# Attention and two dense blocks in one kernel: sets of 384 tokens in place of 288 in the gated block

## The chip, the cores and the metric

The kernel runs on one core of one Trainium2 chip. The metric is the device time of one execution in microseconds; a kernel is timed in several runs, and one execution more is recorded by the hardware profiler, which gives the span from the first to the last instruction, the busy time of each engine and who waited for whom. PE is the matrix engine (PEld its weight loads), DVE, ACT and POOL are the vector, scalar and general engines, SP issues the transfers between the chip's memory and the on-chip buffers.

## What is computed

Attention over 4 batches of 576 tokens with 8 heads of 64, with a mask by blocks of 64 tokens, then two dense blocks on the 2304 x 512 result, all in float32:

```python
scores = scale * np.matmul(q, k.transpose(0, 1, 3, 2))
scores = np.where(mask, scores, -1000000000.0)
attn = softmax(scores)
x = (attn @ v).transpose(0, 2, 1, 3).reshape(B * S, H * D)
x = ((x @ w1) * (x @ w2)) @ w3 @ w_out                 # the gated block, 512 -> 1024 -> 1024 -> 512
h = x @ w_in                                           # the last block, 512 -> 2048 -> 512
out = np.where(h > 0, h, np.exp(np.minimum(h, 0)) - 1) @ w_out2
```

`mask[i, j]` is true where `i // 64 >= j // 64`.

## The kernel before, in words

Precision. A float32 operand is split in two parts for PE, a rounded one and the rest, and a product is made of three matmuls (`PASSES`: high with high, high with low, low with high). A split is a copy on ACT (or a cast on DVE) and a subtraction on POOL or DVE. Weights arrive as 64-bit words and are turned into float32 on ACT, DVE and POOL (`convert`).

Three stages, which overlap:

- *Attention* (`attention`): 16 pairs of heads, four for each batch. For a pair the scores of five groups of queries are made on PE, the maximum on DVE (L611), the exponential on ACT (L616), the transposition on PE (L626), the product with v on PE (L716). The sums' reciprocals go to the chip's memory and come back spread over the partitions as the tile `rr`, in three transfers (L758); POOL multiplies the pair's result, a part of `xy[b]`, by it (L770). `rr` has two buffers (`rr_r`).
- *The gated block* (`block2`). `w3 @ w_out` is multiplied once in advance (`w_product`, L786), so a set of tokens needs the two projections and one product. A set is `T2 = 288` tokens, half a batch; there are eight, and set t needs batch t // 2 alone. First the set's four slices of 128 features are cast and split into `xs` (DVE L827, POOL L832; one buffer, so the next set's `xs` waits for the last projection of this one). Then, for each of eight slices m of the 1024 features: 12 matmuls into `a`, copied by ACT (L899), 12 into `b`, multiplied by that copy on DVE (L904) and split into `g` (ACT L810, POOL L813). `g` has six buffers (`g2_r`). The output is summed in three parts over the slices, `PARTS = ((0,1,2),(3,4,5),(6,7))`: each part makes, for each of four slices n of the output, 3 matmuls for each of its m (L851). The first part is copied over the set's own place in `xy` (ACT L865), the others are added to it (DVE L871). Sets 0 to 2 have one PSUM bank for each of `a`, `b` and `y`, later ones two.
- *The last block* (`round_in`, `part_h`, `part_o`, `post`) works in three rounds of 768 tokens with Strassen's scheme: seven products of sums and differences of operand halves, in matmuls of `T3 = 384` columns (L1130 and L1208). `round_in(r)` makes the inputs `sy`; the result of `part_h` goes through the exponential unit into `ga` or `gb`; `part_o` builds sums of those (`sum_next`, three buffers), splits them (`split_next`, four places) and multiplies. There are six passes j; `part_o(j - 1)` is listed after `part_h(j)`, and the last `part_o` stands alone. Its weights were converted and stored to the chip's memory while the gated block ran.

Order. Nothing is issued directly. Each operation is added to a `Plan` with an engine (or several possible ones), an estimated duration, the buffers that it reads and writes and a priority. `Plan.run` is a list scheduler: it takes for each engine the operation that is ready and has the lowest priority, and issues in that order; the engines run their queues in order and wait for each other by semaphores. Attention's priorities lie below those of the gated block (base `1e4 + 1000 t`), and those below the last block's (`1e5`). The table `TURNS` replaces the priority of some operations, by their number, with values set by hand. Estimated durations, among them the cost of a matmul after one of another kind, the rate of the transfers and whether DVE and POOL hold each other up (`port`), decide the order alone, not what is computed.

Memory that is shared: `gate1` opens the buffers of the last block when attention and the conversions of the gated block's weights are done, `gate2` when the gated block is.

Of the kernel before, what the change touches and what calls it, by code (L numbers as in the profile page):

```python
# [29 lines left out]
T2 = 288  # L30
T3 = 384
BIG = 2.0**100
PARTS = ((0, 1, 2), (3, 4, 5), (6, 7))
# [106 lines left out]
class Op:  # L140
    __slots__ = ("eng", "ways", "us", "fn", "prio", "deps", "n", "ready", "end", "users", "left", "lag", "nbytes", "big")


class Plan:
    LANES = 8
    OVER = {"GATE": 0.0, "PE": 0.0, "DVE": 0.085, "ACT": 0.1, "POOL": 0.04}
    SEEN = {"GATE": 0.0, "PE": 0.055, "DVE": 0.035, "ACT": 0.035, "POOL": 0.08, "SP": 0.03}
# [4 lines left out]
    def add(self, eng, us, fn, r=(), w=(), prio=0.0, port=False, after=(), lag=0.0, nbytes=0, ways=(), big=False):  # L152

        o = Op()
        o.eng, o.us, o.fn, o.prio, o.lag, o.nbytes, o.big = eng, us, fn, prio, lag, nbytes, big
# [33 lines left out]
    def run(self):  # L189
# [11 lines left out]
        was_big = False  # L201
        pipe, port, done, lanes = 0.0, {"DVE": 0.0, "POOL": 0.0}, 0, [0.0] * self.LANES
        while done < len(self.ops):
# [15 lines left out]
            if e == "PE":  # L219
                o.us += 0.09 if o.big and not was_big else 0.0  # L220
                was_big = o.big
# [29 lines left out]
def attention_moe_moe2(  # L251
# [23 lines left out]
    N2, N3 = B * S // T2, B * S // (2 * T3)  # L275
    plan = Plan()
# [186 lines left out]
    rr_r = Ring(pool1, "rr", 2, [P, S], F32)  # L463
# [21 lines left out]
    def attention(n, first_op):  # L485
# [62 lines left out]
        def q_last():  # L548
# [8 lines left out]
            "POOL", 0.6, q_last, r=[(qs, 0)] if whole else [(qs, 0), (qs, 1)], w=[("qb", n % 2)], prio=pr + 1  # L557
# [14 lines left out]
        def group(g, seq):  # L572
# [7 lines left out]
            def scores():  # L580
# [20 lines left out]
                "PE", (4 * w / 2390 if whole else 3 * w * COL) + (0.28 if added else 0.17), scores,  # L601
                r=[*q_keys, *k_keys, "mask"], w=[*sb], prio=pg,
            )
            for h in range(2):
# [23 lines left out]
                add("PE", 0.11 * (g + 1) + 0.09, transposes, r=[p, "ident"], w=[t], prio=pg)  # L628
# [8 lines left out]
        def last_block(seq):  # L637
# [4 lines left out]
            for g in range(2):  # L642

                def scores(g=g):
# [13 lines left out]
                    "PE", (4 * kw / 2390 if whole else 3 * kw * COL) + 0.1, scores,  # L658
                    r=[("qb", n % 2), *k_keys], w=[sb[g]], prio=pg,
# [7 lines left out]
                )  # L667
            add(
                "DVE", 0.16, lambda: nc.vector.tensor_tensor(out=nm(10), in0=nm(8), in1=nm(9), op=ALU.min),
                r=[(st, "nm", 8), (st, "nm", 9)], w=[(st, "nm", 10)], prio=pg,  # L670
            )
            for g in range(2):
                add(
# [290 lines left out]
    def sum_next():  # L964
        b = sums[count("sum", 3)]
        return (lambda: b()[:, :]), (b, 0)
# [514 lines left out]
```

## Time and profile before

| | |
|---|---|
| median of 3 runs | 932.31 us (928.55, 932.61, 932.31) |
| the profiled execution | 929.41 us |
| its span | 927.6 us, 16695 instructions |
| PE, PEld | 901.3 us (97%), 799.0 us (86%) |
| DVE, ACT, POOL | 739.8, 513.2, 533.1 us |
| granted TensorE clock, mean | 0.996 of full speed |

The profile's page gives the busy time of each engine and the costliest groups of instructions: line, engine, operation, what it writes and reads, shape, count, then busy time, mean duration of one, and the idle time before them with what ended it. Matmuls are pipelined, so the records of neighbours overlap. The windows give the same busy times for a stretch of the span. The waits list who waited for whom. The chain follows the work that ended last back from the end, piece by piece.

### The profile page before, as it was taken

To read this page: it belongs to the slowest core of one execution; us is meant where nothing else is said; L and a number is where in the kernel's file an instruction comes from. 1 tells how busy PE (TensorE), PEld (TensorE's weight loads), DVE (VectorE), ACT (ScalarE), POOL (GpSimd) and SP (SyncE) were. 2 spreads that over 40 slices of the span, in tenths; PEclk is the share of its full clock that TensorE was granted. 3 is DMA by queue.
4 is the path that set the end of the run, shared out by engine and by line. 5 is a ranking of instruction groups with operands and counts; after the bars stand their busy time and mean duration, and the time that the engine had idled before them with its cause. 6 is when DMAs were issued, how large, how long until landed. Compare 5 with 4: busy or idle time off the path is not lost.

```text
span 927.6 us, 16695 instructions
## 1 busy us (share of the span) xinstructions
PE 901.3 (97%) x5838; PEld 799.0 (86%) x5838; DVE 739.8 (80%) x1450; ACT 513.2 (55%) x1190; POOL 533.1 (57%) x527
## 2 busy tenths in 40 slices
PE   7998899999999999999999999999999999999997
PEld 3454477888787778999999999999999999999996
DVE  7999889778676675777877768878998789986887
ACT  5857668666565654436354443455644547444552
POOL 6556667554242313578887985336995238961245
PEclk9999999999999999999999999999999999999999
DMA  8765553545222212777666595776789766887665
GB/s 267 242 203 172 171 159 97 180 148 167 79 73 67 69 39 88 249 253 251 219 220 215 170 308 193 232 262 234 247 287 304 264 223 216 308 285 269 213 199 188
DMA packets 100756, 186.24 MB, mean 201 GB/s; under 512 B 8512, under 2 KB 50496, under 8 KB 100672
## 3 DMA queue, kind: packets, MB, share of 16 engines
q1 hardware_dynamic: 100672, 185.18, 61.2%
q8 instruction: 46, 0.75, 0.3%
q14 instruction: 38, 0.31, 0.1%
HBM read 147.85 MB, written 37.30 MB: 200 GB/s over the span
## 4 chain that ended last, share of the span: by engine, by line
PE 71%; DMA 10%; DVE 8%; POOL 4%; issue 3%; ACT 3%; SPq 0%; POOLq 0%; DVEq 0%; ACTq 0%
PE y L851 9%; PE a L887 9%; PE b L887 8%; PE hx L1130 7%; PE ox L1208 7%; PE hz L1130 5%; PE hy L1130 5%; PE oy L1208 5%; PE oz L1208 5%; PE o L716 3%; PE s L590 3%; PE t L626 3%; DMA cr<-w 2%; DMA cr<-w3T 2%; DMA rr<-scr 2%
## 5 line engine op out<-in xcount | busy, mean ns | idle before, releaser
L851 PE MATMUL y<-g,slab_lo 128*128 128x288 f32 x768 | 120.2, 299 | 2.0 <-POOL g L813 2.0
L887 PE MATMUL a<-xs,slab_lo 128*128 128x288 f32 x768 | 117.6, 298 | 0.4 <-ACT af L899 0.3
L887 PE MATMUL b<-xs,slab_lo 128*128 128x288 f32 x768 | 116.7, 297 | 0.4 <-DVE af L904 0.4
L851 PEld LDWEIGHTS y<-g,slab_lo 128*128 128x128 f32 x768 | 107.4, 188 | 3.9 <-POOL g L813 2.2
L887 PEld LDWEIGHTS a<-xs,slab_lo 128*128 128x128 f32 x768 | 106.5, 188 | 2.0 <-ACT af L899 1.0
L887 PEld LDWEIGHTS b<-xs,slab_lo 128*128 128x128 f32 x768 | 106.5, 188 | 1.3 <-DVE af L904 0.6
L1208 PE MATMUL ox<-sp,wout 128*128 128x384 f32 x432 | 86.1, 335 | 0.9 <-DVE sum L1013 0.5
L616 ACT ACTIVATE p<-s,st 128x128 f32<-128x128 f32 (+3 forms) x128 | 67.4, 528 | 35.2 <-DVE st L611 26.7
L1130 PE MATMUL hx<-sy,win 128*128 128x384 f32 x432 | 86.5, 335 | 0.3 <-DVE ga L1013 0.3
L813 POOL TENSOR_TENSOR g<-af,g 128x288 fp32r<-128x288 f32 x64 | 57.6, 902 | 42.4 <-ACT g L810 40.4
L1208 PEld LDWEIGHTS ox<-sp,wout 128*128 128x128 f32 x432 | 75.7, 188 | 1.7 <-ACT sp L1003 0.8
L1130 PEld LDWEIGHTS hx<-sy,win 128*128 128x128 f32 x432 | 75.6, 188 | 1.0 <-DVE ga L1013 0.9
L1003 ACT CAST sp<-sum 128x384 fp32r<-128x384 f32 x72 | 36.7, 513 | 62.6 <-PE ox L1208 24.3
L786 PE MATMUL wps<-full,full 128*128 128x512 f32 x128 | 61.3, 613 | 4.5 <-DVE slab_lo L800 2.6
L611 DVE TENSOR_REDUCE st<-s 128x1 f32<-128x128 f32 (+3 forms) x128 | 61.9, 488 | 4.0 <-PE s L596 0.7
L384 ACT ACTIVATE cr<-cr 128x512 int32<-128x512 uint32 x72 | 49.0, 682 | 28.4 <-DMA cr<-w 19.8
L626 PE MATMUL t<-ident,p 128*128 128x128 f32 x320 | 56.3, 285 | 7.3 <-ACT p L616 4.9
L1208 PE MATMUL oy<-sp,wout 128*128 128x384 f32 x288 | 59.1, 336 | 1.5 <-DVE sp L1004 1.5
L626 PEld LDWEIGHTS t<-ident,p 128*128 128x128 f32 x320 | 37.3, 141 | 26.5 <-ACT p L616 13.5
L1130 PE MATMUL hz<-sy,win 128*128 128x384 f32 x288 | 57.6, 335 | 0.3 <-DMA win<-wsi 0.3
L1208 PE MATMUL oz<-sp,wout 128*128 128x384 f32 x288 | 57.1, 335 | 0.8 <-POOL sp L1004 0.8
L1130 PE MATMUL hy<-sy,win 128*128 128x384 f32 x288 | 57.6, 334 | 0.0
(154 smaller groups left out, 2093.7 us busy)
## 6 DMA issues: line engine op xcount, KB each, us to landing
wout<-wso SPq DMA_DIRECT2D x84, 512.0 KB
cr<-w SPq DMA_DIRECT2D x48, 512.0 KB
win<-wsi SPq DMA_DIRECT2D x24, 1024.0 KB
win<-wsi SPq DMA_DIRECT2D x24, 768.0 KB
cr<-w3T SPq DMA_DIRECT2D x16, 512.0 KB
wsi<-wh SPq DMA_DIRECT2D x8, 896.0 KB
wsi<-wt SPq DMA_DIRECT2D x8, 896.0 KB
wso<-wh SPq DMA_DIRECT2D x8, 896.0 KB
```

What stands on the lines that cost most here:

```text
L384: nc.scalar.activation(out=low, in_=low.bitcast(U32), func=AF.Copy, scale=2.0**-29)
L590: nc.tensor.matmul(sb[h]()[:, 0:w], lhsT=qs()[r, a, g * P:(g + 1) * P], rhs=ks()[r, c, 0:w], start=(x == 0), stop=(x == 2 and not added),)
L611: nc.vector.tensor_reduce(out=nm(c), in_=s()[:, 0:nk], axis=AX.X, op=ALU.max, negate=True)
L616: lambda s=s, c=c, p=p: nc.scalar.activation(out=p()[:, 0:nk], in_=s()[:, 0:nk], func=AF.Exp, bias=nm(c), scale=1.0, accum_out=sm(c)),
L626: nc.tensor.transpose(d[:, j, :], p()[:, j * P:(j + 1) * P], ident)
L786: nc.tensor.matmul(ps(), lhsT=a[:, j, :], rhs=bb, start=(j == 0), stop=(j == KF - 1))
L813: lambda: nc.gpsimd.tensor_tensor(out=g()[:, 1, :], in0=src(), in1=g()[:, 0, :].bitcast(F32), op=ALU.subtract),
L851: nc.tensor.matmul(ps()[:, 0:T2], lhsT=w[:, a, n * P:(n + 1) * P], rhs=gs[m]()[:, c, :], start=(m == ms[0] and q == 0), stop=(m == ms[-1] ...
L887: nc.tensor.matmul(ps()[:, 0:T2], lhsT=w[:, a, u, k, :], rhs=xs()[:, k, c, :], start=(k == 0 and q == 0), stop=(k == KD - 1 and q == 2),)
L1003: add("ACT", act_us(n, True), lambda: nc.scalar.copy(dst(0), src()), r=keys, w=[dkeys[0]], prio=prio)
L1130: nc.tensor.matmul(bk()[:, 0:T3], lhsT=w[:, a, k, :], rhs=s_(c), start=(first and k == 0 and i == 0), stop=(k == 1 and i == 2), skip_group ...
L1208: nc.tensor.matmul(to[n]()[:, 0:T3], lhsT=w[:, a, n * P:(n + 1) * P], rhs=sp(c), start=(first and q == 0 and i == 0), stop=(q == KP - 1 an ...
```

## The change

Sets of 384 tokens: `T2` is 384, there are six sets, and a set that spans two batches (the second and the fifth) is handled in two pieces for its inputs and for its outputs' copies and additions. `PARTS` becomes `((0,1,2),(3,4),(5,6,7))`, the ring of `g` has four buffers, `rr` one, `sums` two; sets 0 and 1 are now those with single banks. Before the last `part_o`, `widen` hands it ten more places for splits, in the slabs of `sy`, and eight more for sums. The planner knows six kinds of matmul and a cost for each change of kind, a lower transfer rate, and three more operations that hold the port; `TURNS` is replaced by a new table.

```diff
-T2 = 288
+T2 = 384
 T3 = 384
-PARTS = ((0, 1, 2), (3, 4, 5), (6, 7))
+PARTS = ((0, 1, 2), (3, 4), (5, 6, 7))
...
 TURNS = {
-    5: -2500.01, 24: -2400.0, 26: -10019.0, 31: -2542.64, 32: -9968.45, 51: -2496.99, 56: -871.07, 57: -10149.67,
...
+    4: -2505.56, 9: -100000.02, 22: -9857.07, 23: -997.98, 36: -3035.53, 41: -2498.87, 65: -2417.38, 69: -2499.99,
...
+    KINDS = {"": 0, "big": 1, "w": 2, "t": 3, "s": 4, "pv": 5, "qb": 6}
+    TURN = (
+        (0, 0, 0, 0, 0, 0, 0),
+        (0, 0, 0, 0.03, 0.085, 0.085, 0.03),
+        (0, 0, 0, 0, 0.094, 0.094, 0.03),
+        (0, -0.08, 0.04, 0.02, 0.14, 0.14, -0.08),
+        (0, 0, 0, 0, 0, 0, 0),
+        (0, 0, 0, 0, 0, 0, 0),
+        (0, 0.01, 0.01, 0, 0.09, 0.09, 0.05),
+    )
...
             if e == "PE":
-                o.us += 0.09 if o.big and not was_big else 0.0
-                was_big = o.big
+                o.us += 0.09 if o.kind in (1, 2) and last not in (1, 2) else 0.0
+                t = max(free[e] + self.TURN[last][o.kind], o.ready)
+                last = o.kind
...
-                pipe = max(pipe, t + 1.8) + o.nbytes / 325e3
+                pipe = max(pipe, t + 1.8) + o.nbytes / 300e3 + 0.05
...
-    rr_r = Ring(pool1, "rr", 2, [P, S], F32)
+    rr_r = Ring(pool1, "rr", 1, [P, S], F32)
...
-    g2_r = Ring(pool2, "g", 6, [P, 2, T2], F32R)
+    g2_r = Ring(pool2, "g", 4, [P, 2, T2], F32R)
...
     def block2(t):
-        b, h2 = divmod(t, 2)
-        c0 = T2 * h2
+        parts = pieces(t)
         xs = xs2_r.next()
-        base = 1e4 + 1000.0 * t
+        base = 1e4 + 1350.0 * t
         fast = -1e4 + t
-        x = xy[b]
         for k in range(KD):
-            src = lambda k=k: x()[:, k, c0:c0 + T2]
...
+            for b, o, n, d0 in parts:
+                x = xy[b]
+                src = lambda k=k, x=x, o=o, n=n: x()[:, k, o:o + n]
+                dst = lambda c, k=k, n=n, d0=d0: xs()[:, k, c, d0:d0 + n]
...
         gs = []
-        few = t < 3
+        few = t < 2
...
-                d = lambda n=n: x()[:, n, c0:c0 + T2]
-                dk = (x, n, "y", h2)
...
+                for b, o, cn, d0 in parts:
+                    x = xy[b]
+                    d = lambda n=n, x=x, o=o, cn=cn: x()[:, n, o:o + cn]
+                    acc = lambda ps=ps, d0=d0, cn=cn: ps()[:, d0:d0 + cn]
+                    dk = (x, n, "y", t)
...
-    sums = [Ring(late1, f"sum{u}", 1, [P, T3], F32, "gate1").next() for u in range(3)]
+    sums = [Ring(late1, f"sum{u}", 1, [P, T3], F32, "gate1").next() for u in range(2)]
...
+    def widen():
+        sx = [
+            chain([f"slab{s}"], "sx", [P, 2, 2, T3], F32R, [b]).next() for s, b in zip((11, 6, 7, 4, 5), sy_s)
+        ]
+        late["sx"] = [(b, u) for b in (*late["sp"], *sx) for u in range(2)]
+        su = [chain(b_tags, "sx", [P, 2, T3], F32, [b], late1, "gate1").next() for b_tags, b in zip(SY_TAGS, sy_l)]
+        late["su"] = [(b, u) for b in su for u in range(2)]
+
     def split_next():
+        if "sx" in late:
+            b, u = late["sx"][count("sx", len(late["sx"]))]
+            return (lambda c: b()[:, u, c, :]), [(b, u, c) for c in range(2)]
...
     def sum_next():
-        b = sums[count("sum", 3)]
+        k = count("su", len(late["su"]) + 2) if "su" in late else 0
+        if k >= 2:
+            b, u = late["su"][k - 2]
+            return (lambda: b()[:, u, :]), (b, u)
+        b = sums[count("sum", 2)]
...
         if j:
             part_o(j - 1)
+    widen()
     part_o(NP * N3 - 1)
```

`pieces(t)`, which the last block had already, cuts the 384 tokens of a set at the border between batches:

```python
def pieces(t):
    a0, found = t * T3, []
    while a0 < (t + 1) * T3:
        b, o = divmod(a0, S)
        n = min(S - o, (t + 1) * T3 - a0)
        found.append((b, o, n, a0 - t * T3))
        a0 += n
    return found
```

## Rows read from the trace of the kernel before

**Rows 1.** The page: each engine's busy time, share of the span, instructions.

```profile
PE 901.3 (97%) x5838; PEld 799.0 (86%) x5838; DVE 739.8 (80%) x1450; ACT 513.2 (55%) x1190; POOL 533.1 (57%) x527
```

**Rows 2.** Windows: stretch, length, busy time of each engine, clock, transfers.

```profile
core 0: us, PE busy (x) PEld busy (x) DVE busy (x) ACT busy (x) POOL busy (x), PEclk, DMA share, GB/s
0.00:125.60 125.60, 113.31 (x531) 57.85 (x531) 108.96 (x215) 85.83 (x200) 77.02 (x85) 0.97 0.67 207
125.60:243.00 117.40, 113.83 (x865) 97.14 (x863) 97.46 (x228) 78.39 (x208) 64.36 (x64) 1.00 0.44 140
243.00:365.00 122.00, 121.30 (x941) 95.92 (x940) 82.80 (x248) 72.20 (x217) 33.98 (x45) 1.00 0.21 63
365.00:893.00 528.00, 524.24 (x3358) 521.88 (x3355) 424.98 (x725) 264.15 (x541) 339.65 (x320) 1.00 0.74 244
403.40:559.00 155.60, 153.25 (x1142) 152.31 (x1141) 116.52 (x181) 74.54 (x144) 132.60 (x126) 1.00 0.72 232
750.00:800.00 50.00, 48.59 (x277) 47.58 (x276) 46.67 (x81) 28.67 (x66) 35.70 (x38) 1.00 0.75 258
893.00:927.60 34.60, 28.58 (x155) 26.21 (x153) 25.61 (x36) 12.64 (x26) 18.07 (x16) 0.99 0.63 203
```

**Rows 3.** The page's groups: the gated block's matmuls, count, busy, mean, idle before.

```profile
L851 PE MATMUL y<-g,slab_lo 128*128 128x288 f32 x768 | 120.2, 299 | 2.0 <-POOL g L813 2.0
L887 PE MATMUL a<-xs,slab_lo 128*128 128x288 f32 x768 | 117.6, 298 | 0.4 <-ACT af L899 0.3
L887 PE MATMUL b<-xs,slab_lo 128*128 128x288 f32 x768 | 116.7, 297 | 0.4 <-DVE af L904 0.4
```

**Rows 4.** The chain in order of time: start, length, what, matmuls in it.

```profile
379.74 3.20 PE b L887 x24
...
588.67 2.08 PE hx L1130 x12
```

**Rows 5.** Groups by shape, DVE, ACT and POOL: the gated block's own.

```profile
L904 DVE TENSOR_TENSOR af<-b,af 128x288 f32<-128x288 f32 x64 | 28.8, 452 | 20.9 <-PE b L887 16.0 <-ACT af L899 4.4
...
L810 ACT CAST g<-af 128x288 fp32r<-128x288 f32 x64 | 27.5, 432 | 34.5 <-DVE af L904 32.5 <-PE y L851 1.6
...
L813 POOL TENSOR_TENSOR g<-af,g 128x288 fp32r<-128x288 f32 x64 | 57.6, 902 | 42.4 <-ACT g L810 40.4 <-DVE sy L1004 1.8
L832 POOL TENSOR_TENSOR xs<-xy,xs 128x288 fp32r<-128x288 f32 x32 | 27.1, 865 | 8.7 <-DVE xs L827 8.6
```

**Rows 6.** Timeline of PE, 402 to 412 us: start, length, what.

```profile
403.19 6.59 PE L851 MATMUL y<-g,slab_lo 128*128 128x288 f32 x48
409.62 0.96 PE L887 MATMUL a<-xs,slab_lo 128*128 128x288 f32 x6
```

**Rows 7.** Timeline of POOL, 402 to 412 us.

```profile
405.23 2.11 POOL L1375 TENSOR_TENSOR wt<-wt,wh 128x256 fp32r<-128x256 f32 x2
407.30 1.56 POOL L832 TENSOR_TENSOR xs<-xy,xs 128x288 fp32r<-128x288 f32 x2
```

**Rows 8.** The normalizations (L770): duration least, median, most; first and last start.

```profile
L770 POOL TENSOR_TENSOR xy<-xy,rr x16: 1409/1422/1737, 47.5 to 365.9; 128x576 f32<-128x576 f32 x16
```

**Rows 9.** Waits of PE, 893 to 927.6 us: total, times, longest.

```profile
PE oy L1208 <- DVE sp L1004: 1.5, 3, 1.0
PE ox L1208 <- DVE sum L1013: 0.5, 1, 0.5
PE ox L1208 <- DVE sp L1004: 0.4, 1, 0.4
```

**Rows 10.** Timeline of PE, 122 to 128 us: the gated block's first matmuls.

```profile
125.59 1.84 PE L887 MATMUL a<-xs,slab_lo 128*128 128x288 f32 x12
```

**Rows 11.** Timeline of POOL, 234 to 244 us: the normalization of pair 7.

```profile
237.11 1.42 POOL L770 TENSOR_TENSOR xy<-xy,rr 128x576 f32<-128x576 f32 x1 [6.49 <-DVE st L611]
```

**Rows 12.** Groups of PE between 125.6 and 243 us: the gated block's matmuls.

```profile
L887 PE MATMUL a<-xs,slab_lo 128*128 128x288 f32 x174 | 27.2, 299 | 0.4 <-ACT af L899 0.3
L887 PE MATMUL b<-xs,slab_lo 128*128 128x288 f32 x174 | 26.5, 299 | 0.0
L851 PE MATMUL y<-g,slab_lo 128*128 128x288 f32 x132 | 22.7, 303 | 0.0
```

More of the change, by code (lines that the diff above doesn't have):

```diff
@@ L140 @@
 class Op:
-    __slots__ = ("eng", "ways", "us", "fn", "prio", "deps", "n", "ready", "end", "users", "left", "lag", "nbytes", "big")
+    __slots__ = ("eng", "ways", "us", "fn", "prio", "deps", "n", "ready", "end", "users", "left", "lag", "nbytes", "kind")
 class Plan:
@@ L150, in __init__, with add @@
         self.ops, self.writer, self.readers, self.filler = [], {}, {}, None
-    def add(self, eng, us, fn, r=(), w=(), prio=0.0, port=False, after=(), lag=0.0, nbytes=0, ways=(), big=False):
+    def add(self, eng, us, fn, r=(), w=(), prio=0.0, port=False, after=(), lag=0.0, nbytes=0, ways=(), kind=""):
         o = Op()
-        o.eng, o.us, o.fn, o.prio, o.lag, o.nbytes, o.big = eng, us, fn, prio, lag, nbytes, big
+        o.eng, o.us, o.fn, o.prio, o.lag, o.nbytes, o.kind = eng, us, fn, prio, lag, nbytes, self.KINDS[kind]
         o.ways = {e: x for e, *x in ((eng, us, fn, port), *ways)}
@@ L200, in run @@
                     ready[e].append(o)
-        was_big = False
+        last = 0
         pipe, port, done, lanes = 0.0, {"DVE": 0.0, "POOL": 0.0}, 0, [0.0] * self.LANES
@@ L275, in attention_moe_moe2 @@
     N2, N3 = B * S // T2, B * S // (2 * T3)
+    assert T2 == T3
     plan = Plan()
@@ L556, in attention @@
         add(
-            "POOL", 0.6, q_last, r=[(qs, 0)] if whole else [(qs, 0), (qs, 1)], w=[("qb", n % 2)], prio=pr + 1
+            "POOL", 0.6, q_last, r=[(qs, 0)] if whole else [(qs, 0), (qs, 1)], w=[("qb", n % 2)], prio=pr + 1, port=True
         )
@@ L600, in group @@
             add(
-                "PE", (4 * w / 2390 if whole else 3 * w * COL) + (0.28 if added else 0.17), scores,
-                r=[*q_keys, *k_keys, "mask"], w=[*sb], prio=pg,
+                "PE", (4 * w / 2390 if whole else 3 * w * COL) + (0.28 if added else 0.21), scores,
+                r=[*q_keys, *k_keys, "mask"], w=[*sb], prio=pg, kind="s",
             )
@@ L626, in transposes @@
                         nc.tensor.transpose(d[:, j, :], p()[:, j * P:(j + 1) * P], ident)
-                add("PE", 0.11 * (g + 1) + 0.09, transposes, r=[p, "ident"], w=[t], prio=pg)
+                add("PE", 0.109 * (g + 1), transposes, r=[p, "ident"], w=[t], prio=pg, kind="t")
                 pt = pts[g // 2]
@@ L657, in last_block @@
                 add(
-                    "PE", (4 * kw / 2390 if whole else 3 * kw * COL) + 0.1, scores,
-                    r=[("qb", n % 2), *k_keys], w=[sb[g]], prio=pg,
+                    "PE", (4 * kw / 2390 if whole else 3 * kw * COL) + 0.09, scores,
+                    r=[("qb", n % 2), *k_keys], w=[sb[g]], prio=pg, kind="qb",
                 )
@@ L669, in last_block @@
                 "DVE", 0.16, lambda: nc.vector.tensor_tensor(out=nm(10), in0=nm(8), in1=nm(9), op=ALU.min),
-                r=[(st, "nm", 8), (st, "nm", 9)], w=[(st, "nm", 10)], prio=pg,
+                r=[(st, "nm", 8), (st, "nm", 9)], w=[(st, "nm", 10)], prio=pg, port=True,
             )
@@ L686, in tr4 @@
                     nc.tensor.transpose(d[:, j, :], p()[:, j * P:(j + 1) * P], ident)
-            add("PE", 0.48, tr4, r=[(p, 0), (p, 1), "ident"], w=[t], prio=pg)
+            add("PE", 0.436, tr4, r=[(p, 0), (p, 1), "ident"], w=[t], prio=pg, kind="t")
             evac(
@@ L694, in last_block @@
             add(
-                "PE", 0.16, lambda: nc.tensor.transpose(t1()[0:D, 0:P], p()[:, 512:576], ident),
-                r=[(p, 1), "ident"], w=[t1], prio=pg,
+                "PE", 0.109, lambda: nc.tensor.transpose(t1()[0:D, 0:P], p()[:, 512:576], ident),
+                r=[(p, 1), "ident"], w=[t1], prio=pg, kind="t",
             )
@@ L723, in pv @@
                 r += [(pt, "q"), pts[2], (vt, 1)]
-            add("PE", (0.8, 2.3)[c], product, r=r, w=[o], prio=pg)
+            add("PE", (0.8, 2.353)[c], product, r=r, w=[o], prio=pg, kind="pv")
             x = xy[b]
@@ L745, in attention @@
         add("POOL", 0.15, lambda: nc.gpsimd.memset(st()[:, 41:64], 0.0), w=[(st, "rest")], prio=pr)
-        add("DVE", 0.85, recip, r=[(st, "rest"), *((st, "sm", c) for c in range(10))], w=[(st, "rs"), rs], prio=pr + 6)
+        add("DVE", 0.85, recip, r=[(st, "rest"), *((st, "sm", c) for c in range(10))], w=[(st, "rs"), rs], prio=pr + 6, port=True)
         def keep_sums(b):
@@ L789, in w_product @@
                 "PE", 0.86, mm,
-                r=[full_keys(W3_S, i % RW)[j // 4], full_keys(WO_S, j // 2)[j % 2]], w=[ps], prio=prio, big=True,
+                r=[full_keys(W3_S, i % RW)[j // 4], full_keys(WO_S, j // 2)[j % 2]], w=[ps], prio=prio, kind="w",
             )
@@ L805, in attention_moe_moe2, with pieces @@
     xs2_r = Ring(pool2, "xs", 1, [P, KD, 2, T2], F32R)
-    g2_r = Ring(pool2, "g", 6, [P, 2, T2], F32R)
+    g2_r = Ring(pool2, "g", 4, [P, 2, T2], F32R)
     a2_r = Ring(pool2, "af", 2, [P, T2], F32)
+    def pieces(t):
+        a0, found = t * T3, []
+        while a0 < (t + 1) * T3:
+            b, o = divmod(a0, S)
+            n = min(S - o, (t + 1) * T3 - a0)
+            found.append((b, o, n, a0 - t * T3))
+            a0 += n
+        return found
     def split_g(g, src, key, n, prio):
@@ L817, in block2 @@
     def block2(t):
-        b, h2 = divmod(t, 2)
-        c0 = T2 * h2
+        parts = pieces(t)
         xs = xs2_r.next()
-        base = 1e4 + 1000.0 * t
+        base = 1e4 + 1350.0 * t
         fast = -1e4 + t
-        x = xy[b]
         for k in range(KD):
-            src = lambda k=k: x()[:, k, c0:c0 + T2]
-            add(
-                "DVE", 0.32, lambda k=k, src=src: nc.vector.tensor_copy(xs()[:, k, 0, :], src()),
-                r=[(x, k, "n")], w=[(xs, k, 0)], prio=fast, port=True,
-            )
-            add(
-                "POOL", 0.79,
-                lambda k=k, src=src: nc.gpsimd.tensor_tensor(
-                    out=xs()[:, k, 1, :], in0=src(), in1=xs()[:, k, 0, :].bitcast(F32), op=ALU.subtract
-                ),
-                r=[(x, k, "n"), (xs, k, 0)], w=[(xs, k, 1), (x, k, "s", h2)], prio=fast, port=True,
-            )
+            for b, o, n, d0 in parts:
+                x = xy[b]
+                src = lambda k=k, x=x, o=o, n=n: x()[:, k, o:o + n]
+                dst = lambda c, k=k, n=n, d0=d0: xs()[:, k, c, d0:d0 + n]
+                add(
+                    "DVE", 0.15 + n * 0.00052, lambda src=src, dst=dst: nc.vector.tensor_copy(dst(0), src()),
+                    r=[(x, k, "n")], w=[(xs, k, 0, d0)], prio=fast, port=True,
+                )
+                add(
+                    "POOL", 0.17 + n * 0.00215,
+                    lambda src=src, dst=dst: nc.gpsimd.tensor_tensor(
+                        out=dst(1), in0=src(), in1=dst(0).bitcast(F32), op=ALU.subtract
+                    ),
+                    r=[(x, k, "n"), (xs, k, 0, d0)], w=[(xs, k, 1, d0), (x, k, "s", t)], prio=fast, port=True,
+                )
         gs = []
-        few = t < 3
+        few = t < 2
         abanks, bbanks, ybanks = ((5,), (6,), (7,)) if few else ((5, 0), (6, 1), (7, 3))
@@ L858, in y_part @@
                         r=[(gs[m], 0), (gs[m], 1), *((slab_buf[W_S + m // 2], y, m % 2) for y in range(2))],
-                        w=[ps], prio=base + (46, 90, 95)[part] + n, lag=LAG, big=True,
+                        w=[ps], prio=base + (46, 90, 95)[part] + n, lag=LAG, kind="big",
                     )
-                d = lambda n=n: x()[:, n, c0:c0 + T2]
-                dk = (x, n, "y", h2)
-                if part == 0:
-                    add(
-                        "ACT", act_us(T2), lambda d=d, ps=ps: nc.scalar.copy(d(), ps()[:, 0:T2]),
-                        r=[ps], w=[dk, (x, n, "s", h2)], prio=fast,
-                    )
-                else:
-                    add(
-                        "DVE", dve_us(T2),
-                        lambda d=d, ps=ps: nc.vector.tensor_tensor(out=d(), in0=ps()[:, 0:T2], in1=d(), op=ALU.add),
-                        r=[ps], w=[dk], prio=fast,
-                    )
+                for b, o, cn, d0 in parts:
[3 more added lines that the diff above has]
+                    dk = (x, n, "y", t)
+                    if part == 0:
+                        add(
+                            "ACT", act_us(cn), lambda d=d, acc=acc: nc.scalar.copy(d(), acc()),
+                            r=[ps], w=[dk, (x, n, "s", t)], prio=fast,
+                        )
+                    else:
+                        add(
+                            "DVE", dve_us(cn),
+                            lambda d=d, acc=acc: nc.vector.tensor_tensor(out=d(), in0=acc(), in1=d(), op=ALU.add),
+                            r=[ps], w=[dk], prio=fast,
+                        )
         for m in range(KF):
@@ L892, in proj @@
                     add(
-                        "PE", 6 * T2 * COL + 0.025, mm, r=[*wk, *((xs, k, c) for k in (k0, k0 + 1) for c in range(2))],
-                        w=[ps], prio=pr, lag=LAG, big=True,
+                        "PE", 6 * T2 * COL + 0.01, mm, r=[*wk, *((xs, k, c, p_[3]) for k in (k0, k0 + 1) for c in range(2) for p_ in parts)],
+                        w=[ps], prio=pr, lag=LAG, kind="big",
                     )
@@ L925, in attention_moe_moe2 @@
     win_r = slabs((8, 9, 10), "win", [P, 4, 2, NH], F32R)
+    SY_TAGS = [[f"sy{u}_0"] for u in range(4)]
     sy_l = [Ring(late1, f"sy{u}", 1, [P, 2, T3], F32R, "gate1").next() for u in range(4)]
     sy_s = [slabs((s,), "sy", [P, 2, 2, T3], F32R).next() for s in (11, 6, 7, 4, 5)]
-    sums = [Ring(late1, f"sum{u}", 1, [P, T3], F32, "gate1").next() for u in range(3)]
+    sums = [Ring(late1, f"sum{u}", 1, [P, T3], F32, "gate1").next() for u in range(2)]
     wout_r = Ring(late1, "wout", 4, [P, 2, 2, NH], F32R, "gate1")
@@ L943, in stage3 @@
         late["cp"] = xy_buf(0, "cp", (P, 6, T3))
-        late["n"] = dict.fromkeys(("sp", "sum", "ht"), 0)
+        late["n"] = dict.fromkeys(("sp", "sum", "ht", "sx", "su"), 0)
     def count(name, n):
-        late.setdefault("n", dict.fromkeys(("sp", "sum", "ht"), 0))
+        late.setdefault("n", dict.fromkeys(("sp", "sum", "ht", "sx", "su"), 0))
         late["n"][name] += 1
         return (late["n"][name] - 1) % n
+    def widen():
[5 more added lines that the diff above has]
+        late["su"] = [(b, u) for b in su for u in range(2)]
     def split_next():
+        if "sx" in late:
+            b, u = late["sx"][count("sx", len(late["sx"]))]
+            return (lambda c: b()[:, u, c, :]), [(b, u, c) for c in range(2)]
         k = count("sp", 4)
@@ L990, in sy @@
         return (lambda c: b()[:, kt, c, :]), [(b, kt, c) for c in range(2)]
-    def pieces(t):
-        a0, found = t * T3, []
-        while a0 < (t + 1) * T3:
-            b, o = divmod(a0, S)
-            n = min(S - o, (t + 1) * T3 - a0)
-            found.append((b, o, n, a0 - t * T3))
-            a0 += n
-        return found
     def split(src, keys, dst, dkeys, n, prio):
@@ L1023, in y @@
         def y(ps, k, d0, n):
+            t = 2 * r + (ps is pb)
             b, o = next((b, o + d0 - p0) for b, o, m, p0 in ps if p0 <= d0 < p0 + m)
-            return (lambda: xy[b]()[:, k, o:o + n]), [(xy[b], k, "y", h) for h in range(2) if o < (h + 1) * T2 and o + n > h * T2]
+            return (lambda: xy[b]()[:, k, o:o + n]), [(xy[b], k, "y", t)]
         def whole(ps):
@@ L1139, in part_h @@
                     "PE", 6 * T3 * COL + 0.01, mm, r=[(wb[x // 4], 0), *xkeys(x, 0), *xkeys(x, 1)], w=[bk],
-                    prio=pr, lag=LAG, big=True,
+                    prio=pr, lag=LAG, kind="big",
                 )
@@ L1215, in part_o @@
                         "PE", 3 * T3 * COL + 0.01, mm, r=[(wb, 0), *spk], w=[to[n]],
-                        prio=1e5 + 1000 * (j + 1) + 34 * (KP * x + q) + 17 * n, lag=LAG, big=True,
+                        prio=1e5 + 1000 * (j + 1) + 34 * (KP * x + q) + 17 * n, lag=LAG, kind="big",
                     )
```

112 rows, old and new, of the table TURNS are left out of this document.

## The prediction

> **What bounds the kernel now.** I read the page first: PE is busy for 97% of the span, DVE for 80% [rows 1]. An average hides stages, so next come the windows, cut where the work changes [rows 2]. The reader is to compare PE with the length of each stretch. From 365 to 893 us PE is idle for 3.8 us in all, and PEld (the weight loads, which show gaps that the overlapping matmul records hide) is as full: there the end is set by how many matmuls stand in the queue and by what each costs. In the first 125.6 us PE has 12.3 us of gaps, in the next two stretches, where attention and the gated block share PE, 4.3 us. The last stretch has 6.0 us.
>
> **The sum** is made against the profiled execution, 929.41 us (span 927.6 and 1.8 around it). It lies 2.9 us under the median of the runs shown, 932.31, and within their spread of 4 us, so about 0.5% is what a measurement of this kernel can tell from no change.
>
> **Fewer, wider matmuls.** The gated block now issues, per set, 8 slices x 2 projections x 12 matmuls and 8 x 12 for its output: 288, in 8 sets 2304, the 768 + 768 + 768 of [rows 3]. Six sets make it 1728, of 384 columns; the columns in total are the same. The price of one is not the mean in the groups (299 ns), in which pipelined matmuls overlap, but their share of the chain of waits, where a piece lasts until the next begins [rows 4]: 24 matmuls of 288 columns take 3.20 us, 133.3 ns each; 12 of 384 columns, in the stage behind, take 2.08 us, 173.3 ns each. The difference, 40.0 ns for 96 columns, is 0.417 ns for a column, so 288 columns are 120.0 ns and 13.3 ns stay for each matmul whatever its width. 576 matmuls fewer give 576 x 13.3 = 7.7 us. 1440 of the 2304 lie where PE never rests; for the others, in the stretches with 4.3 us of gaps, I take the gain whole too, because PE is still the fullest engine there. Bounds: 4.8 us (the share of the last five sets alone) to 7.7.
>
> What is left over in these rows is 13.3 ns for each matmul. The Trainium skill (TensorE: Matmul & The Clock Gate, section "Back-to-back issue gap") gives the distance at full clock as N/2.4 + 2.5 ns, by which the saving would be 576 x 2.5 = 1.4 us and the time 6.3 us later than I forecast. Both of the measured distances stand 10.8 ns above that formula, so this trace does not agree with its constant.
>
> **The other engines of the block.** Two of the six sets span two batches and are handled in two pieces, so there are 8 pieces as there were 8 sets: the subtractions into xs stay 32 [rows 5] and the casts with them, the output's copies and adds 32 and 64. The multiplications, copies and splits of g become 48 in place of 64, each a third longer: some fixed parts saved on DVE, ACT and POOL. POOL is 85% busy between 403 and 559 us, DVE 75% [rows 2]; PE is ahead of both, so I book nothing.
>
> **Four buffers of g in place of six, parts (0,1,2), (3,4), (5,6,7).** Slice 7 takes the buffer of slice 3, so its split waits until the second part has been read, and that part can no longer stand behind the last projection as cover. At a set's end in the trace PE does 48 output matmuls from 403.19 to 409.62, 6.4 us, while DVE and POOL make the next xs [rows 6]. Now 36 of 173.3 ns are left, 6.24 us, the first of which need slices 5 and 6 alone while slice 7 is split. POOL was not late by itself: it began the first xs subtraction at 407.30, behind other work [rows 7]. Bounds per set end: nothing, or what one split costs, ACT 0.43 and POOL 0.90 for 288 columns [rows 5], a third more of each being 1.8 us as an estimate. For the three ends behind attention I take the shortfall of cover, 3 x 0.2 = 0.6 us; earlier ends have attention as cover.
>
> **One rr buffer in place of two.** The next pair's three fetches wait for this pair's normalization, and loads behind them on SP's queue wait as well. The 16 normalizations of 1.42 us lie between 47.5 and 365.9 [rows 8], some 20 us apart on average, so a buffer is free long before it is wanted: nothing; bound from above 1.4 us where two pairs end together. That a new fetch goes first would need a faster chain, so below nothing I expect no gain.
>
> **Two sums in place of three.** In the last stage a sum is made (DVE), split (ACT, then DVE or POOL) and read. The two changes of round form up to three at once; the stretch from 750 to 800 us, around one of them, has 1.4 us of PE gaps [rows 2]. Taken: nothing; bounds 0 to 2 x 1.4 = 2.8 us.
>
> **More splits and sums for the last part.** The closing output pass may now prepare 14 splits (4 before) and 10 sums (3 before). It waits for just these: 1.5 + 0.5 + 0.4 = 2.4 us on sp and sum [rows 9]. The inputs are there earlier, ACT is only 12.6 of 34.6 us busy; DVE with 25.6 is the limit [rows 2]. Taken: all 2.4 us; bounds 0 and 2.4. The other 3.6 us of the 6.0 stay: they lie behind the last matmul and are an addition and a store.
>
> **The order laid anew.** The planner's prices change (switches between kinds of matmul, DMA speed, port shared by DVE and POOL) and the table of hand-set turns is replaced. No row prices that. Loads, their bytes and queue stay; they only go in another order. The bound below is that half of the 12.3 + 4.3 = 16.6 us of gaps before 365 us goes, the bound above is rival 2. Taken: nothing. One gap of 2.0 us behind a split (y waits for g [rows 3]) I also leave, since the smaller ring may make its like again.
>
> **Sum:** 929.4 - 7.7 - 2.4 + 0.6 = **919.9 us**. Its own range from the bounds: 912 to 926.
>
> **Rivals.**
> 1. *The new order also fills the gaps before 365 us.* For it: 16.6 us of them, though PE is not the limit there and DVE was 87% busy in the first stretch [rows 2], which speaks against getting many back. Half: 919.9 - 8.3 = 911.6. Chance 0.17.
> 2. *A hole after the first set.* Set 1 now contains 192 tokens of batch 1, so it needs all four pairs of that batch; before, it needed batch 0 alone. Set 0 starts at 125.59 [rows 10], batch 1's last normalization at 237.11 [rows 11]; with xs behind it set 1 could start at about 243. Until then PE did 174 + 174 + 132 = 480 matmuls of the block [rows 12], 192 above set 0's 288: 25.6 us of work that would not be there yet. Set 0 is longer by 12.8, so 12.8 us are missing, if neither batch 1 is finished earlier nor batch 2's attention is brought forward. DVE's 97.5 of 117.4 us [rows 2] makes that tight; that pair 8 needs nothing of it speaks against the hole. 919.9 + 12.8 = 932.7. Chance 0.14.
> 3. *The smaller ring of g becomes the wait* (this one ends slower). Place: the end of each set, where slice 7's split waits for the second part, and xs stands behind it on POOL. Price: a split of 1.8 us plus the product before it (DVE 0.45 for 288 columns [rows 5], 0.6 as an estimate), 2.4 us, and as much again in the middle of a set where slice 4 waits for the first part: up to 12 x 2.4 = 28.8. It decides from 10 us, four or five uncovered waits of twelve. For it: such a wait was 2.0 us once, even with six buffers [rows 3]. Against: slice 5's projections, 24 x 0.1733 = 4.2 us, can cover the middle one. With seven: 919.9 + 16.8 = 936.7. Chance 0.10.
> 4. *A matmul's cost goes by columns alone*, so 8 sets and 6 sets cost the same: 919.9 + 7.7 = 927.6. The prices of 133.3 and 173.3 ns speak against it. Chance 0.04. By the Trainium skill's formula named above, which lies between this and the forecast, it would be 926.2; the same rows speak against it, and it has no more than half of this chance.
> 5. *The change doesn't do what it says*: straddling sets or slices that stay as they were. The counts would show it; the diff leaves no room. Chance 0.01.
>
> **How the numbers follow.** The forecast has 0.54. The range, not quite symmetric, reaches from rival 1 with a little more, 909, to rival 2, 933; rival 3 lies outside it, and so does a better rival 1. Faster by over 0.5% means below 927.6, against the median: the forecast's 0.54, rival 1's 0.17, and small versions of rivals 2 and 3, 0.04: 0.75. Within 0.5%: rivals 4 and 5 and most of 2: 0.15. Slower: rival 3 and the rest of 2: 0.10.
>
> **What would show it.** Right: L851's and L887's counterparts with 576 matmuls each, 12 in 2.08 us of the chain; the block's stretch without attention as full as now; in the last 30 us no wait of PE on sp or sum. Wrong: PE or PEld below 95% right after the first set, with the multiplication by rr or xs as releaser (rival 2); y waiting on g, or a on xs, at the end of each set (rival 3); new waits on sums where the rounds change. If 12 matmuls of the block take more than 2.1 us, the main term is wrong.

## The result and the profile after

The changed kernel takes 916.95 us, median of four runs (915.47 to 918.98); the runs of before beside them have a median of 931.33. The ratio is 0.9851 with an interval of 0.9818 to 0.9884: faster by 1.5%. The forecast was 919.9, its own range 912 to 926. The total is close; the steps that made it are not, as the rows show.

The page's groups of the gated block, after, which answer to [rows 3]:

```profile
L899 PE MATMUL y<-g,slab_lo 128*128 128x384 f32 x576 | 116.5, 343 | 0.7 <-DVE xy L922 0.7
L938 PE MATMUL b<-xs,slab_lo 128*128 128x384 f32 x576 | 113.1, 342 | 0.8 <-DVE af L955 0.8
L938 PE MATMUL a<-xs,slab_lo 128*128 128x384 f32 x576 | 112.4, 341 | 0.0
```

The counts are as forecast, 576 each. The mean of one is not: 341 to 343 ns, where the same shape in the last block has 335 (page of the same run):

```profile
L1189 PE MATMUL hx<-sy,win 128*128 128x384 f32 x432 | 86.8, 335 | 0.1
```

The chain of waits says it without overlap, as in [rows 4]; two pieces of after, one of the block and one of the last block:

```profile
144.62 2.12 PE a L938 x12
...
601.05 2.08 PE ox L1267 x12
```

12 matmuls of the block take 2.12 us, 176.7 ns each; the last block's take the 173.3 on which the forecast stood. The windows of after, cut where the work changes, beside [rows 2]:

```profile
core 0: us, PE busy (x) PEld busy (x) DVE busy (x) ACT busy (x) POOL busy (x), PEclk, DMA share, GB/s
0.00:122.00 122.00, 112.08 (x543) 57.56 (x543) 106.44 (x213) 89.12 (x210) 81.41 (x88) 1.00 0.68 217
122.00:236.00 114.00, 111.18 (x751) 90.89 (x752) 96.41 (x239) 77.31 (x209) 62.54 (x65) 1.00 0.48 149
236.00:350.00 114.00, 114.00 (x822) 91.35 (x821) 75.82 (x222) 65.08 (x202) 31.19 (x38) 1.00 0.19 56
350.00:885.00 535.00, 529.22 (x3010) 524.53 (x3009) 433.14 (x705) 264.88 (x531) 355.78 (x323) 1.00 0.73 242
885.00:916.10 31.10, 26.26 (x150) 25.62 (x149) 23.14 (x29) 8.48 (x18) 22.72 (x19) 0.96 0.65 220
```

The block begins at 122 instead of 125.6 us and attention ends at 350 instead of 365. PE's gaps ahead of that are 9.9 + 2.8 + 0.0 = 12.7 us, where they were 16.6. The granted clock of the first stretch is 1.00 in place of 0.97 [rows 2]; in the trace of before it fell to the lower level twice there, the second time right behind a wait of PE of 2.6 us (on `slab_lo`, shown further down). That can be worth 0.03 x 125.6 = 3.8 us at most, as an estimate, and no run separates it. Busy time hides more than it shows here, because the end of a matmul is modelled. So I summed, from both traces, the time from each PE instruction's start to the next one's start, by what the instruction is; a wait falls to the instruction before it. In us:

| | before | after | with 32 bytes (below) |
|---|---|---|---|
| gated block | 322.8 | 319.3 | 311.4 |
| attention | 172.4 | 160.8 | 161.7 |
| `w3 @ w_out` and warm-up | 70.5 | 71.9 | 69.7 |
| last block | 356.1 | 357.1 | 356.2 |
| ahead of the first, behind the last start | 5.9 | 7.0 | 6.6 |
| span | 927.6 | 916.1 | 905.6 |

Attention's row fell by 11.6 us and the block's by 3.5, where the forecast had 7.7 for the block and nothing for attention. The rows are shares and not causes: an order that puts a block matmul between two of attention's moves time from one row to the other, as shown further down.

### The profile page after: what moved, and what is told of

Same layout as the page of the kernel before. It is cut to its first block, busy times and chain, and to the rows that moved or that the text cites. A ratio compares the mean times of both kernels' runs of the same rounds, so it can differ in the third digit from the quotient of the medians.

```text
span 916.1 us, 15391 instructions
## 1 busy us (share of the span) xinstructions
PE 892.7 (97%) x5268; PEld 790.0 (86%) x5268; DVE 734.9 (80%) x1406; ACT 504.9 (55%) x1168; POOL 553.6 (60%) x529
## 4 chain that ended last, share of the span: by engine, by line
PE 71%; DVE 10%; DMA 9%; ACT 3%; issue 3%; POOL 2%; SPq 1%; ACTq 0%; DVEq 0%; POOLq 0%
PE a L938 10%; PE b L938 10%; PE y L899 9%; PE hx L1189 7%; PE ox L1267 6%; PE hz L1189 5%; PE hy L1189 5%; PE oz L1267 4%; PE oy L1267 4%; PE o L754 3%; DMA win<-wsi 3%; PE t L664 3%; PE s L628 3%; DMA cr<-w 2%; DMA cr<-w3T 2%
## 5 line engine op out<-in xcount | busy, mean ns | idle before, releaser
L899 PE MATMUL y<-g,slab_lo 128*128 128x384 f32 x576 | 116.5, 343 | 0.7 <-DVE xy L922 0.7
L938 PE MATMUL b<-xs,slab_lo 128*128 128x384 f32 x576 | 113.1, 342 | 0.8 <-DVE af L955 0.8
L938 PE MATMUL a<-xs,slab_lo 128*128 128x384 f32 x576 | 112.4, 341 | 0.0
L654 ACT ACTIVATE p<-s,st 128x256 f32<-128x256 f32 (+3 forms) x128 | 67.4, 529 | 29.6 <-DVE st L649 23.6
L860 POOL TENSOR_TENSOR g<-af,g 128x384 fp32r<-128x384 f32 x48 | 53.5, 1120 | 32.8 <-ACT g L857 31.4
L1267 PE MATMUL ox<-sp,wout 128*128 128x384 f32 x372 | 73.2, 334 | 0.0
L649 DVE TENSOR_REDUCE st<-s 128x1 f32<-128x256 f32 (+3 forms) x128 | 61.7, 489 | 5.7 <-PE s L634 2.5
L429 ACT ACTIVATE ct<-cr 128x512 f32<-128x512 f32 x59 | 39.8, 677 | 28.2 <-POOL wt L452 12.6
L1189 PEld LDWEIGHTS hz<-sy,win 128*128 128x128 f32 x288 | 50.5, 188 | 4.2 <-DMA win<-wsi 4.2
L754 PE MATMUL o<-pt,v 128*64 128x320 f32 (+4 forms) x448 | 52.7, 367 | 1.0 <-ACT pt L518 1.0
```

The lines of the kernel that those rows point to most:

```text
L429: nc.scalar.activation(out=t().bitcast(F32), in_=words()[1].bitcast(F32), func=AF.Abs)
L649: nc.vector.tensor_reduce(out=nm(c), in_=s()[:, 0:nk], axis=AX.X, op=ALU.max, negate=True)
L654: lambda s=s, c=c, p=p: nc.scalar.activation(out=p()[:, 0:nk], in_=s()[:, 0:nk], func=AF.Exp, bias=nm(c), scale=1.0, accum_out=sm(c)),
L754: nc.tensor.matmul(o()[D * h:D * h + D, lo:cols], lhsT=vt()[0:kn, j, D * h:D * h + D], rhs=p, start=(j == 0), stop=(j == last),)
L860: lambda: nc.gpsimd.tensor_tensor(out=g()[:, 1, :], in0=src(), in1=g()[:, 0, :].bitcast(F32), op=ALU.subtract),
L899: nc.tensor.matmul(ps()[:, 0:T2], lhsT=w[:, a, n * P:(n + 1) * P], rhs=gs[m]()[:, c, :], start=(m == ms[0] and q == 0), stop=(m == ms[-1] ...
```

## Experiments: the price of a matmul

In the built programs the block's moving operands, `xs` and `g`, start at addresses that leave 32 when divided by 64, before as after; those of the last block are multiples of 64. Reserving a few bytes above these buffers moves them (`af`, and later `gb`, move with them). The order stays: not one of PE's instructions changes its place in the traces of the two runs with 32 bytes.

```diff
+    pad = ctx.enter_context(tc.tile_pool(name="pad", bufs=1, side="right"))
+    pad.tile([P, 8], F32, name="pad")
     ph2 = ExitStack()
```

**32 bytes in the changed kernel.**

> The changed kernel with 32 bytes reserved above the gated block's buffers, so that xs and g begin at a multiple of 64 bytes instead of 32 past one; nothing else moves, and the order is the same. Theory P (the place of the moving operand sets the 177 ns of a matmul of the gated block): its 384-column matmuls fall to the 173.3 ns of the last block, 1728 x 3.6 ns = 6.2 us less than the changed kernel. Theory E (other engines' traffic or the PSUM banks set it): 177 ns stay, no change in time.

Measured: 910.27 us, ratio to before 0.980 (0.9773 to 0.9827). All its runs (907.36 to 911.55 us) lie under those of the changed kernel, though the intervals of the two ratios overlap by a little (0.9818 to 0.9827). The chain in this run:

```profile
143.34 2.08 PE a L940 x12
...
243.73 2.08 PE b L940 x12
```

173.3 ns, and the block's share falls by 7.9 us. 1728 x 3.3 ns, the difference of the mean distances between two of the block's matmuls with no wait between them (176.6 and 173.3), are 5.7; the time fell by 6.7 us by the medians and 4.7 by the ratios. Theory P's numbers hold, those of E do not. This version is faster than both kernels.

**32 bytes in the kernel before.**

> The kernel before with the same 32 bytes. Theory P, with the cost by columns alone once the operand is in place: 288 columns fall from 133.3 to 173.3 x 288/384 = 130.0 ns, 2304 x 3.3 ns = 7.7 us less, if PE sets the end throughout. The prediction's reading (13.3 ns fixed for every matmul whatever its place): 133.3 ns stay and the time stays within 0.3%.

Measured: 928.58 us, ratio 0.9994 (0.9979 to 1.0009). The chain:

```profile
197.79 1.60 PE b L889 x12
241.88 1.59 PE b L889 x12
```

Still 133 ns. With both shapes in place, 133.1 and 173.3 as means, the prediction's reading stands: 13 ns for each matmul beside 0.417 ns for a column. At 288 columns the wrong place costs nothing, at 384 it costs 3.3 ns. That is why no row of before could show it: the one row for 384 columns was of buffers at another place.

**64 bytes, a control,** and **96 bytes.**

> Control: 64 bytes reserved, so xs and g move by 64 bytes and stay 32 past a multiple of 64. Theory P: 177 ns as in the changed kernel, time within 0.3% of it. If the reserved bytes act in another way than by the place within 64 bytes, it would fall like the run with 32.

Measured, in a single run: 916.44 us, the time of the changed kernel, as expected; but the matmuls are only partly slow. Their mean is near 174 ns in most stretches of 20 us up to 320, 176.7 between 360 and 440, and 173.3 from 520 on. Three other traces with the operands at the place of the changed kernel (the one without `widen` and the two with an empty table, below) have 176.6.

> The changed kernel with 96 bytes reserved: xs and g begin at a multiple of 64 again, as with 32 bytes, but at another place within 512. Theory P: 173.3 ns for the gated block's matmuls throughout and about 910 us. If 32 bytes was a lucky place and not the multiple of 64: something between 173 and 177 ns, as with 64 bytes.

Measured, in a single run: 908.32 us; 173.3 to 173.7 ns from 360 us on, but around 175 in most stretches before. So at a multiple of 64 the block's own stretch ran at the fast price in both runs, and 32 beside it the price can be slow or change between two values within one execution. That the place acts is shown by the pair with 32 bytes; that the multiple of 64 is the whole rule is not. What switches the price is open.

## Experiments: the wider last part

```diff
-    widen()
     part_o(NP * N3 - 1)
```

> The changed kernel without the call of widen: the last output pass has four places for splits and two for sums. The prediction's term: 2.4 us longer than the changed kernel, with waits of PE on sp and sum in the last 30 us. Rival (the order alone fills the end): within 0.5 us.

Measured: 921.05 us, ratio 0.9922 (0.9904 to 0.994): 4.1 us above the changed kernel by the medians, 6.6 by the two ratios, and the intervals do not meet. All waits of PE in the last 33 us of this run:

```profile
PE oy L1267 <- DVE sp L1062: 2.9, 1, 2.9
```

The changed kernel has none in its last 31 us. The last block's share is 360.7 in place of 357.1. The term was of the right kind and smaller than what it brings: 3.6 us by the rows, 4.1 by the medians, 6.6 by the ratios.

## Experiments: the rings

```diff
-    g2_r = Ring(pool2, "g", 6, [P, 2, T2], F32R)
+    g2_r = Ring(pool2, "g", 4, [P, 2, T2], F32R)
-    rr_r = Ring(pool1, "rr", 2, [P, S], F32)
+    rr_r = Ring(pool1, "rr", 1, [P, S], F32)
-    sums = [Ring(late1, f"sum{u}", 1, [P, T3], F32, "gate1").next() for u in range(3)]
+    sums = [Ring(late1, f"sum{u}", 1, [P, T3], F32, "gate1").next() for u in range(2)]
```

(and `count("sum", 2)`). All three in the kernel before:

> The kernel before with the changed kernel's rings alone: four buffers of g, one rr, two sums; sets, parts and table as they were. The prediction's terms: 0.6 us for g, nothing for rr and sums, so within 0.3% of the kernel before. Rival 3 of the prediction (the ring of g becomes the wait): 5 us or more longer, with y waiting on g; a loss on the sums would show as waits of PE on sum or sp between 565 and 893 us.

Measured: 948.77 us, ratio 1.0184 (1.0148 to 1.0221), where the prediction had 0.6 us. Then g alone and the sums alone:

> The kernel before with four buffers of g in place of six, all else as it was. If g is what made the three smaller rings together 17 us longer: 6 us or more longer than the kernel before, in the gated block's share of PE's time. The prediction's term: 0.6 us.

> The kernel before with two sums in place of three, all else as it was. If the sums are what made the three smaller rings together longer: 6 us or more, in the last block's share of PE's time. The prediction's term: nothing, with a bound of 2.8 us.

Measured: 941.95 us, 1.0097 (1.0063 to 1.0132), and 941.39, 1.0092 (1.006 to 1.0125). Each costs about 9 us, and the two together leave nothing of the 1.84% for `rr`. In the first the block's share is 330.1 (322.8 before), in the second the last block's 362.4 (356.1). PE's waits between 375 and 560 us with four buffers of g; before, the same view had two, 2.0 us on `g` [rows 3] and 0.4 on `af`:

```profile
PE y L851 <- DVE xy L871: 1.6, 7, 0.5
PE y L851 <- ACT xy L865: 0.7, 1, 0.7
PE a L887 <- POOL xs L832: 0.5, 1, 0.5
```

Not one is on `g`. They are on the output's additions and on xs. The ring is felt one engine further back, where ACT's split into `g` waits until PE has read what the buffer held; over the whole run (before: once, 1.6 us):

```profile
ACT g L810 <- PE y L851: 10.0, 6, 2.8
```

With two sums no wait of PE on a sum is listed; its wait in the last block's `hx` for DVE's `ga` went from 0.3 to 2.0 us. And the order has moved: against the trace of before, PE's sequence differs at 1310 of its 5838 places with four buffers of g, at 303 with two sums. That is the limit of these two runs. A smaller ring changes the scheduler's order while the table of turns still holds values set for the old one, and, as the next runs show, losing the table's help alone costs as much. How much the rings cost under an order made for them stays open.

## Experiments: the order

Both kernels with an empty table:

```diff
-TURNS = {
-    4: -2505.56, 9: -100000.02, 22: -9857.07, 23: -997.98, 36: -3035.53, 41: -2498.87, 65: -2417.38, 69: -2499.99,
...
+TURNS = {}
```

> The changed kernel with an empty table of turns: the planner's own priorities order everything, its new prices stay. Theory O (most of what the change gained beyond the matmuls is the order, above all where attention's matmuls stand among the others): at least 8 us longer than the changed kernel, the loss in attention's share of PE's time (161 us from start to start in the changed kernel, 172 before). Rival S (the sets, buffers and prices carry the gain, the table little): less than 3 us longer.

> The kernel before with an empty table of turns, the other side of the pair. Theory O: its loss against the kernel before is smaller than the changed kernel's loss against itself or alike, and the two flat kernels lie within about 5 us of each other. Rival S: the flat changed kernel stays 10 us or more ahead of the flat kernel before.

Measured: 925.46 us, 0.9925 (0.9895 to 0.9954), and 940.39, 1.0092 (1.0058 to 1.0126). The changed kernel loses 8.5 us by the medians (6.9 by the ratios), attention's share going back from 160.8 to 173.2, as theory O said; the block's goes the other way, from 319.3 to 314.2. The kernel before loses alike, 8.1 us (8.6), with attention's share where it was, 171.8. But the two kernels with empty tables lie 15 us apart, which was rival S's number. Both tables are worth about the same, so the table is not what separates the kernels. Sets, buffers or prices are:

```diff
-    TURN = (
...
+    TURN = ((0,) * 7,) * 7
...
-                pipe = max(pipe, t + 1.8) + o.nbytes / 300e3 + 0.05
+                pipe = max(pipe, t + 1.8) + o.nbytes / 325e3
...
-                add("PE", 0.109 * (g + 1), transposes, r=[p, "ident"], w=[t], prio=pg, kind="t")
+                add("PE", 0.11 * (g + 1) + 0.09, transposes, r=[p, "ident"], w=[t], prio=pg, kind="t")
...
```

(the other durations and the three `port` marks likewise; the reverse of it for the kernel before).

> The changed kernel, empty table, and all of the planner's prices as before (no cost for a change of kind, durations, port, transfer rate): only sets, parts, rings and the wider last part are new. Theory B (the buffers and sets carry it): within 3 us of the changed kernel with an empty table, 925.5 us, so still 12 us or more ahead of the kernel before with an empty table, 940.4. Theory K (the planner's prices carry it): 5 us or more longer than 925.5, with more transposes followed by scores.

> The other corner: the kernel before, empty table, with the new prices. Theory B: within 3 us of 940.4 us. Theory K: 5 us or more shorter, at 935 or less.

Measured, with the two from above, ratios to the kernel before:

| empty table | prices of before | new prices |
|---|---|---|
| sets and buffers of before | 1.0092 | 0.9935 (0.9913 to 0.9958), 926.28 us |
| changed | 0.9996 (0.9975 to 1.0017), 930.84 us | 0.9925 |

The new prices take 1.6% from the kernel before and 0.7% from the changed one; theory K's numbers hold in both, its sign hardly (53 transpositions followed by scores of 64 rows against 49). Sets and buffers take 1.0% under the old prices and nothing that can be told under the new ones. So with an empty table the estimates by which the planner orders its queues, which compute nothing, are worth as much to the kernel before as the whole change. Summed from start to start, they take 6.5 us from the row of `w3 @ w_out` and the warm-up and 6.6 from the block's, leave attention's (171.8 and 171.5) and add 2.8 to the last block's. The first 120 us show a part. The kernel before, empty table, old prices, and under it the same with new ones:

```profile
0.00:120.00 120.00, 105.05 (x508) 53.83 (x509) 107.41 (x201) 84.64 (x196) 75.41 (x85) 0.99 0.65 208
```

```profile
0.00:120.00 120.00, 110.73 (x524) 56.96 (x525) 109.32 (x207) 87.37 (x201) 77.59 (x86) 0.99 0.68 214
```

PE's gaps fall from 15.0 to 9.3 us, and over the whole span its waits on the exponential, in the same order:

```profile
PE t L581 <- ACT p L571: 8.2, 11, 1.6
```

```profile
PE t L592 <- ACT p L582: 2.5, 5, 0.7
```

Which of the prices does it was not tried: they were taken together.

## Why the prediction was right, and where it was wrong

**Fewer, wider matmuls (7.7 us): the law held, its input did not.** The step that failed is the price of 173.3 ns for the 1728 matmuls, read from the last block's rows. In the changed kernel's buffers it is 176.6, so undisturbed the matmuls take 1728 x 176.6 = 305.2 us against 2304 x 133.3 = 307.1: 2.0 us. The other 5.7 came when the operands were moved by 32 bytes. The prediction had set its own test, "If 12 matmuls of the block take more than 2.1 us, the main term is wrong", and 2.12 failed it. Rival 4, cost by columns alone, was nearer in its amount than the forecast and wrong in its reason: 133.1 and 173.3 ns, both at a good place, are not in the proportion of 288 to 384. The Trainium skill's formula that the prediction holds against these prices (TensorE: Matmul & The Clock Gate, section "Back-to-back issue gap") is given there for an isolated matmul, not for a stream with a weight load before each. In this case's traces the warm-up's matmuls of 512 bf16 columns keep to it (215 to 216 ns from start to start from 6 us on, at a granted clock of 1.00; by the formula 215.8); the block's, at 10.8 ns above, do not.

**The order (taken: nothing) was the step that failed most.** Rival 1 had put half of 16.6 us, from gaps that busy time shows. Those fell by 3.9; 2.6 of it is one wait of the kernel before, which the changed one does not have, and which stands in attention's row because a transposition came ahead of it:

```profile
PE wps L786 <- DVE slab_lo L800: 2.6, 1, 2.6
```

More lay where no gap is listed. Part of it is which kind of matmul follows which. From start to start a transposition lasts 28 ns when one of the block's matmuls follows and 203 when scores of 64 rows do; a matmul of the block lasts 88 ns longer before such scores (265 in place of 177). So a block matmul put between the two makes 28 + 265 out of 177 + 203 or so, some 87 ns less each time. Transpositions followed by such scores went from 42 to 12: 30 x 0.087 = 2.6 us. Without the table they are 49 in the changed kernel, so this part is the table's work. In attention's row it counts 30 x 0.175 = 5.3 us, because the 88 ns fall to the block's; so the 11.6 us are not a net gain. Of them, some 3.7 us were not traced to a cause.

The net worth of the order is in the four corners. New prices bring 6.6 us with the changed sets (0.9996 to 0.9925) and 14.6 with those of before (1.0092 to 0.9935); the new table brings 1.7 us less than the old one did, by the ratios, which is within the noise.

**The rings (0.6 us, 0, 0).** In the kernel before they cost 9 us each for g and sums, so the terms were too small by far there. In the changed kernel the stretch from 350 to 885 us has 5.8 us of gaps, against 3.8 in the stretch of [rows 2]; what the rings cost beside listed gaps, no run separates. The largest of PE's waits in it is on transfers of weights, not on a sum:

```profile
PE hz L1189 <- DMA win<-wsi: 3.2, 3, 1.4
PE b L938 <- DVE af L955: 0.8, 2, 0.6
PE y L899 <- DVE xy L922: 0.7, 2, 0.4
```

No wait of PE on `g` is listed, so rival 3 did not come. ACT's split into `g` waits for PE, somewhat more than in the kernel before with four buffers, but the waits of PE behind it that are listed are the 0.8 us on `af`:

```profile
ACT g L857 <- PE y L899: 13.4, 8, 2.6
```

**The last part (2.4 us)** was right in kind and under-sized: it measured 3.6 to 6.6 us.

**Rival 2, the hole after the first set,** did not come. Batch 1's last normalization starts at 217.44 instead of 237.11 [rows 11], so the batch was finished earlier, one of the two ways out that the rival named, and set 1 did not even wait for it. PE's and POOL's timelines of after:

```profile
217.24 1.29 PE L938 MATMUL b<-xs,slab_lo 128*128 128x384 f32 x6
```

```profile
217.44 1.43 POOL L808 TENSOR_TENSOR xy<-xy,rr 128x576 f32<-128x576 f32 x1 [0.57 <-ACT pt L518]
```

A projection's first six matmuls need slices 0 and 1 alone, which come from the batch's first two pairs. The prediction had made the whole batch a condition of the first matmul; that step was wrong, and with it the 12.8 us. (By its own prices set 0 is longer by 288 x 40.0 ns = 11.5 us and not 12.8, so the hole would have been 14.1.) PE was filled with the first set's outputs and with attention, with 2.8 us of gaps in 114.

The sum came out near because errors met: 5.7 us too much for the matmuls, and nothing for an order that brought several us. That is luck, and the corners show how much hangs on what is held fixed: sets and buffers bring 8.9 us under the old prices (1.0092 to 0.9996), near the 9.5 of the sum, and 0.9 under the new ones. The range of 912 to 926 does not follow from the bounds that the prediction names; added up they reach from 911 to 934.

## What to carry to other kernels

A price per instruction belongs to the row's buffers as well as to its shape: before a term rests on a shape from another stage, compare where the operands lie, and where it matters try 32 bytes of padding, which cost nothing here and gave 0.5%. Where a scheduler computes the order, an edit of a buffer is also an edit of the order; pairs of runs with the hand-set part removed show how much of the time hangs on it. Here new estimates alone were worth as much as the change of the tiling, and with them in place the tiling brought nothing more that can be told.

## What the runs showed of the hardware that was not expected

- A matmul of 384 float32 columns, rounded, one weight load each, takes 173.3 ns from start to start in the run that moves its operand by 32 bytes to a multiple of 64, and 176.6 in the changed kernel, 32 past one; 288 columns take 133.3 and 133.1 at the two places. In one run 32 past, the price went between 174, 176.7 and 173.3 during the execution; in one at another multiple of 64 it was around 175 before 360 us and 173.3 to 173.7 behind.
- A 128 x 128 transposition lasts, from its start to the next instruction's, 28 ns before a matmul of 128 rows, 203 ns before scores of 64 rows and 109 ns before another transposition. A block matmul of 384 columns lasts 177 ns before its like and 265 before scores of 64 rows.
